# A written order for the opening of a packed-attention, MLP and MoE-attention kernel

## The chip, the cores and the metric

The kernel runs on one core of one Trainium2 chip. The metric is the device time of one execution, in microseconds. The engines are TensorE (PE, its weight loads PEld), VectorE (DVE), ScalarE (ACT), GpSimd (POOL) and SyncE (SP), which issues the DMAs in the kernel before.

## The reference, cut to what matters

```python
# packed attention: B=8, H=8 heads, S=576, D=64, 32 packed rows a head
p_packed = softmax(scale * p @ k.T) @ v            # 32 x 64 a head
x = softmax(scale * q @ p_packed.T) @ p_packed     # 576 x 64 a head, heads side by side: 576 x 512
# gated MLP, weights in float64
h = gelu_tanh(x @ w_in); u, v = h[..., :512], h[..., 512:]
v_n = (v - mean) / sqrt(var + 1e-6) * g_ln
gated = u * (w_sg @ v_n + b_sg)
x = x + gated @ w_out
# MoE of 4 attention experts, 2 of them taken by the gate of each row
w = softmax over the two largest of x @ w_gate
out = sum over e of mask * w * (causal_softmax(scale * (x wq[e]) (x wk[e]).T) @ (x wv[e]) @ wo[e])
```

## The kernel before, in words

The eight batches are run one behind the other, as a pipeline of written steps. The x of the packed attention is never formed: the second softmax (a2, 576 rows by 8 heads of 32 packed rows) is kept, and each weight that x would meet is multiplied by the packed heads instead. So `wp_mm` forms w_in times the packed heads (for v, f = 1, and for u, f = 0), `v_tiles` and `u_tile` are a2 times that, `bdw` does the same for the weights of q, k, v and the gate, and `qk` and `vlog` add a part from the gated MLP output (`qk_gated`, with w_out folded into the weights once by `fold`) and a part from a2 (`qk_packed`). Nearly all of these products are split into high and low parts (`lo_part` subtracts the high part), three passes each.

The opening (`startup`, L1129 to L1222) is batch 0 with all that is done once. w_in and w_out come as float64 words; `from_f64_top`, `from_f64_abs` and `from_f64_low` (L148 to L163) make float32 of them, five VectorE operations and one of ScalarE's for each of 12 pieces of 128 x 512. w_out is turned and folded into the q, k, v and gate weights, four pieces (`prep_w_out`, `fold`, `fold_out`); w_sg is turned and split, five pieces (`prep_w_sg`). Batch 0's k and q are turned on TensorE (`transpose_in`), those of later batches by DMA transposes of 16-bit halves, one head at a time (`turn`), stored (`keep`), read back as planes (`planes`) and joined by GpSimd (`join`). The list `TURN` holds these steps, and `tick` issues the next of them. `keep_w_all` (L217) copies the unfolded weights within DRAM in 20 DMAs, so that `load_w` can bring them back in each batch for `bdw`.

What sets the order: in `startup` only TensorE runs in the order written (`manual_schedule`, L1225); the other engines and SP's DMAs are ordered by a planner from its own costs. From L1227 on TensorE and SP follow the written order, and VectorE, ScalarE and GpSimd are the planner's. `front` (L1039) holds the v and u products, `back` (L1051) everything else of a batch, mixed with the steps of the previous batch's expert attention: S0 to S9 are scores (two heads of experts each), T0 to T9 the transposes of their softmax, y0 to y4 the products with v, o0 to o4 those with wo. Steps of the next batch's packed attention stand between them: K and Q joins, s and r the first and second packed scores, a the transposes, p and P the packed heads. All PSUM tiles come from four slots of two banks (`pd`).

Of the kernel before, what the change touches and what calls it, by code (L numbers as in the profile page):

```python
# [7 lines left out]
F32 = mybir.dt.float32  # L8
# [18 lines left out]
def packed_attention_mlp_moe_kernel(  # L27
# [35 lines left out]
    NB = {"A": 4, "B": 10, "C": 4, "D": 12, "a": 3, "p": 1, "T": 4, "nat": 2, "x": 2, "t": 4, "v2": 1, "y": 1, "W": 2}  # L63
# [44 lines left out]
    nc.sync.dma_start(g_bc, dap(moe_g_ln, 0, [[0, P], [1, DM]]))  # L108
# [39 lines left out]
    def from_f64_top(raw, dst):  # L148
        hw, top = words(raw)[:, :, 1], dst.bitcast(I32)
        nc.vector.tensor_scalar(top, hw, 3, 0x3FFFFFF8, op0=OP.logical_shift_left, op1=OP.bitwise_and)  # L150
        nc.vector.scalar_tensor_tensor(top, hw, -0x40000000, top, op0=OP.bitwise_and, op1=OP.bitwise_or)

    def from_f64_abs(raw):
        hw = words(raw)[:, :, 1].bitcast(F32)
        nc.scalar.activation(hw, hw, AF.Abs)

    def from_f64_low(raw, dst, pw):
        lw, hw, top = words(raw)[:, :, 0], words(raw)[:, :, 1], dst.bitcast(I32)
        f = pw.bitcast(F32)
        nc.vector.tensor_scalar(pw, top, -0x800000, None, op0=OP.bitwise_and)  # L160
        nc.vector.scalar_tensor_tensor(f, lw.bitcast(U32), 2.0 ** -52, f, op0=OP.mult, op1=OP.mult)
        nc.vector.tensor_tensor(f, f, dst, op=OP.add)
        nc.vector.scalar_tensor_tensor(dst, hw.bitcast(F32), LEAST_F64, f, op0=OP.is_ge, op1=OP.mult)  # L163
# [3 lines left out]
    def load_w_sg(c):  # L167
        if c < 4:
            if c % 2 == 0:
                wst["t"] = slot("A", name="wst")  # L170
            wst[c] = wst["t"][:, (c % 2) * S:(c % 2) * S + S]
        else:
            wst[c] = slot("p", name="wst")
        nc.sync.dma_start(wst[c][:TOK[c]], moe_w_sg[c * P:c * P + TOK[c], :])
# [54 lines left out]
    def prep_w_sg(c):  # L229
        n = TOK[c]  # L230
        st = wst[c]
        pw = pd("wsgT")
        pt, pl = pw[:, 0, :], pw[:, 1, :]
        for a in range(4):
            nc.tensor.transpose(pt[:, a * P:a * P + n], st[:n, a * P:(a + 1) * P], ident[:n, :n])
        nc.tensor.transpose(pl[:64, 0:n], st[:n, 512:576], ident[:n, :n])
        cols = slice(c * P, c * P + n)
        src = pt.rearrange("p (a t) -> p a t", a=4)[:, :, :n]
        act_copy(w_sg[0][:, 0:4, cols], src)
        lo_part(nc.vector, w_sg[1][:, 0:4, cols], src, w_sg[0][:, 0:4, cols])  # L240
        act_copy(w_sg[0][:64, 4, cols], pl[:64, :n])
        act_copy(w_sg[0][64:P, 4, cols], pl[:64, :n])
        lo_part(nc.vector, w_sg[1][:64, 4, cols], pl[:64, :n], w_sg[0][:64, 4, cols])
# [18 lines left out]
    woT = {}  # L262

    wos = {}

    def wo_top(c):
        wos[c] = slot("B", w=512, name="wo")
        from_f64_top(raw_out[c], wos[c])
        from_f64_abs(raw_out[c])

    def wo_low(c):
        from_f64_low(raw_out[c], wos[c], slot("t", I32, 512, name="pw"))

    def prep_w_out(c):

        wo = wos.pop(c)
        pt = pd("woT")[:, 0, :]
        for j in range(4):
# [985 lines left out]
```

## Time and profile before

| | us |
|---|---|
| median of 3 runs (lowest, highest) | 879.61 (877.87, 881.14) |
| the profiled execution | 878.9 |
| its span, first to last instruction | 877.0 |
| TensorE busy | 825.4 |
| VectorE busy | 583.3 |
| ScalarE busy | 424.7 |
| GpSimd busy | 188.4 |

The 40 slices of the page are 21.9 us each; a digit is the busy share in tenths. A busy TensorE is the modelled span of its matmuls, so it says that the stream did not stop, not that it ran at its peak. The clock row is the granted share of TensorE's full clock, in tenths.

### The profile page before, as it was taken

Reading aid. Unit: us, or ns where it says so; the run is one execution under the profiler, and the core shown is the slowest. Engines: PE = TensorE matmul, PEld = TensorE weight load, DVE = VectorE, ACT = ScalarE, POOL = GpSimd, SP = SyncE. Lnnn points to the kernel's source line nnn. Section 1 sums busy time; section 2 is a strip of 40 time slices with the busy share of each in tenths; the row PEclk is TensorE's granted clock in tenths of the full one; section 3 lists DMA queues with packets and bytes.
Section 4 is the critical chain, followed back from the end, with each engine's and each line's share of the span. In section 5 each row is a group of like instructions: output and inputs, shape, how many; then the busy total and the mean of one; then the engine's idle time right before and its main releaser. Section 6 shows DMA issues by size and latency. Waiting matters only on the chain.

```text
span 877.0 us, 19165 instructions
## 1 busy us (share of the span) xinstructions
PE 825.4 (94%) x7517; PEld 697.9 (80%) x7517; DVE 583.3 (67%) x1387; ACT 424.7 (48%) x973; POOL 188.4 (21%) x272
## 2 busy tenths in 40 slices
PE   4687988999999999999999999999999999999987
PEld 2356877788888888888789888888789888888965
DVE  6766644876577674877477665867488566866265
ACT  2356332565436542655346552655346543745245
POOL 0002051312332151303322141404222141300000
PEclk9798889999999999999999999999999999999989
DMA  9886673537445563548245563549263660100001
GB/s 307 229 208 176 143 234 86 146 88 224 114 99 143 140 188 86 154 109 231 76 130 116 148 188 83 154 111 237 69 153 89 171 178 7 74 13 26 19 1 55
DMA packets 178725, 114.08 MB, mean 130 GB/s; under 512 B 118282, under 2 KB 166666, under 8 KB 175820
## 3 DMA queue, kind: packets, MB, share of 16 engines
q1 hardware_dynamic: 178636, 112.87, 48.0%
q8 instruction: 59, 0.97, 0.5%
q14 instruction: 30, 0.25, 0.1%
HBM read 68.26 MB, written 29.63 MB: 112 GB/s over the span
## 4 chain that ended last, share of the span: by engine, by line
PE 75%; DVE 5%; ACT 2%; issue 1%; POOL 0%; ACTq 0%; DVEq 0%; POOLq 0%
PE vs L744 10%; PE qk L789 10%; PE y L968 6%; PE vlog L832 6%; PE qk L801 5%; PE v L676 5%; PE o L999 5%; PE sc L885 4%; PE u L726 4%; PE aTp L939 4%; PE vlog L836 3%; PE sc L915 2%; PE wp L625 1%; PE aTp L953 1%; PE s L448 1%
## 5 line engine op out<-in xcount | busy, mean ns | idle before, releaser
L744 PE MATMUL vs<-w_sg,vnh 128*128 128x288 f32 x512 | 92.8, 304 | 0.7 <-DVE w_sg L85 0.7
L789 PE MATMUL qk<-gh,w_qk 128*128 128x288 f32 x512 | 92.7, 304 | 0.0
L789 PEld LDWEIGHTS qk<-gh,w_qk 128*128 128x128 f32 x512 | 76.2, 193 | 10.6 <-issue 7.1
L82 ACT ACTIVATE aT<-aTp 128x512 f32<-128x512 f32 (+4 forms) x160 | 60.9, 434 | 44.1 <-PE aTp L939 36.2
L744 PEld LDWEIGHTS vs<-w_sg,vnh 128*128 128x128 f32 x512 | 75.7, 191 | 5.3 <-issue 3.0
L416 POOL COPY kT<-kp 128x576 uint16<-128x576 uint16 x56 | 48.0, 921 | 147.4 <-DMA kp<-turned_k 98.1
L898 ACT ACTIVATE at<-sc,nm 128x256 f32<-128x256 f32 (+3 forms) x128 | 66.3, 524 | 26.7 <-DVE nm L889 21.1
L691 POOL TENSOR_TENSOR rstd<-rstd,mhalf 128x1 f32<-128x1 f32 x40 | 36.4, 917 | 152.8 <-DVE rstd L690 152.8
L968 PE MATMUL y<-aT,v 128*64 128x128 f32 (+2 forms) x960 | 61.6, 267 | 0.2 <-ACT aT L82 0.2
L902 DVE TENSOR_SCALAR at<-at,sm,gw 128x256 f32<-128x256 f32 (+3 forms) x128 | 60.1, 511 | 2.3
L832 PE MATMUL vlog<-w_vg,gh 128*128 128x260 f32 (+1 forms) x320 | 60.8, 287 | 0.0
L968 PEld LDWEIGHTS y<-aT,v 128*64 128x64 f32 (+1 forms) x960 | 48.4, 140 | 14.1 <-issue 7.6
L819 POOL CAST last_q<-qk 64x64 fp32r<-64x64 f32 x64 | 14.9, 233 | 196.6 <-ACT qk L809 103.1
L789 PE MATMUL qk<-gl,w_qk 128*128 128x288 f32 x256 | 55.6, 299 | 0.0
L744 PE MATMUL vs<-w_sg,vnl 128*128 128x288 f32 x256 | 55.3, 298 | 0.0
L889 DVE TENSOR_REDUCE nm<-sc 128x2 f32<-128x256 f32 (+3 forms) x64 | 52.6, 822 | 1.7
L999 PE MATMUL o<-w_o,y 128*128 128x512 f32 x192 | 52.5, 408 | 0.5 <-ACT y L978 0.5
L832 PEld LDWEIGHTS vlog<-w_vg,gh 128*128 128x128 f32 (+1 forms) x320 | 47.4, 178 | 3.5 <-issue 2.8
L885 PE MATMUL sc<-qk 64*128 64x256 f32 (+3 forms) x384 | 47.4, 352 | 0.0
L416 POOL COPY qT<-qp 128x576 uint16<-128x576 uint16 x56 | 44.6, 870 | 11.0 <-DMA qp<-turned_q 11.0
L939 PE MATMUL aTp<-ident,at 128*128 128x128 f32 x320 | 46.6, 277 | 0.0
L899 DVE TENSOR_SCALAR sm<-sm 128x2 f32<-128x2 f32 x64 | 16.4, 256 | 44.9 <-ACT at L898 44.5
(208 smaller groups left out, 1927.9 us busy)
## 6 DMA issues: line engine op xcount, KB each, us to landing
w_in<-kept_in SPq DMA_DIRECT2D x14, 1024.0 KB
w_qk<-kept_qk SPq DMA_DIRECT2D x8, 1024.0 KB
out_dram<-ot SPq DMA_DIRECT2D x32, 256.0 KB
turned_k<-kx SPq DMA_DIRECT2D x56, 144.0 KB
turned_q<-qx SPq DMA_DIRECT2D x56, 144.0 KB
kp<-turned_k SPq DMA_DIRECT2D x56, 144.0 KB
qp<-turned_q SPq DMA_DIRECT2D x56, 144.0 KB
v<-in_v_dram SPq DMA_DIRECT2D x56, 128.0 KB
```

The costliest lines, as they stand in the source:

```text
L82: nc.scalar.activation(o, i, AF.Copy, scale=scale)
L416: nc.gpsimd.tensor_copy(w[:, i], t[:, i].rearrange("p h n -> p (h n)"))
L744: nc.tensor.matmul(pt[:, h, :HALF], s["vn", c][x][:, cols], w_sg[y][:, c, hs(h)], start=(c, x, y) == (0, 0, 0), stop=False)
L789: nc.tensor.matmul(o[:, h, :], W["w_qk"][y][:, m, cols], s["g", m][x][:, hs(h)], start=first and (m, x, y) == (0, 0, 0), stop=not first an ...
L832: nc.tensor.matmul(pt[:n, ci, :260], s["g", m][x][:, c * P:c * P + n], W["w_vg"][y][:, m, :], start=(m, x, y) == (0, 0, 0), stop=False)
L885: nc.tensor.matmul(pt[:, e, :L], qs[x][r, j * P:L], ks[y][r, :L], start=i == 0, stop=i == 2)
L889: nc.vector.tensor_reduce(nm, pt[:, :, :L], axis=AX.X, op=OP.max, negate=True)
L898: nc.scalar.activation(ats[e][:, :L], pt[:, e, :L], AF.Exp, bias=nm[:, e:e + 1], accum_out=sm[:, e:e + 1])
L902: nc.vector.tensor_scalar(ats[e][:, :L], ats[e][:, :L], sm[:, e:e + 1], s["w"][:, j, 2 * pr + e:2 * pr + e + 1], op0=OP.mult, op1=OP.mult)
L939: nc.tensor.transpose(pt[:, e, c * P:c * P + P], ats[e][:, c * P:c * P + P], ident)
L968: nc.tensor.matmul(pt[64 * e:64 * e + 64, pr * w:pr * w + w], s["v2"][:m, c, col:col + D], s["aT", pr, e, j][c][:m, :], start=c == 0, stop ...
L999: nc.tensor.matmul(pt, ys[:, pr, x, :], W["w_o"][y][:, pr, :], start=i == 0, stop=i == 5)
```

## The change

The opening becomes one list, `ORDER`, of some 300 steps, and TensorE, VectorE, ScalarE, GpSimd and SP all issue their instructions in its order. For that the functions are cut into steps of one engine each. Step names: `D...` are loads (wo and in pieces of w_out and w_in, f and piece), `...t p l g a` the parts of a conversion (upper, lower, join, guard, absolute), K, Kc, s, sm, se, n, aT, aTc, pp, ppc, ppT, ppTc, S, St, Sx, Ss, Se, Su, Sn, Sb, ah, al the packed attention of batch 0, wT, wTc, fa, fb, fh, fl the turn, fold and split of w_out, w, wh, wv, wl, wH, wL those of w_sg, wp, wph, wpl w_in times the packed heads, v, g, b, pw, c, vh, vl the v tiles, vs the products with w_sg, u, ug, go, gh, gl the gated part, `A` the first step for batch 1, `t` one tick, kw the copies within DRAM, ki the stores of converted w_in, `F` the planes of batch 1's k, `W` the reload of the q, k, v weights. Where a name ends in a small letter of the pair l/L, s/S the work is GpSimd's.

With that, GpSimd takes the join of each conversion, the subtraction of the maximum in batch 0's second softmax, and the low parts of a2, of w_sg and of the normed v in batch 0; for the last two ScalarE first writes a copy from PSUM or a scaled v to SBUF. The 20 copies within DRAM are issued on ScalarE's queue. Heads are turned in pairs, so 8 turns and 8 stores a batch for 16. Behind batch 0 `first_back`, and for later batches `later_back`, take the place of the first part of `back`: scores come in pairs (S1 S3, S5 S4, S6 S7, S8 S9, S0 S2), T1 stands behind two vs products, the second packed scores and `wp_mm` for the next v stand ahead of the last v-logit products.

```diff
-    def from_f64_low(raw, dst, pw):
...
+        def lower():
+            nc.vector.tensor_scalar(pw, top, -0x800000, None, op0=OP.bitwise_and)
+            nc.vector.scalar_tensor_tensor(f, lw.bitcast(U32), 2.0 ** -52, f, op0=OP.mult, op1=OP.mult)
+        def join(eng):
+            eng.tensor_tensor(f, f, dst, op=OP.add)
+        def guard():
+            nc.vector.scalar_tensor_tensor(dst, hw.bitcast(F32), LEAST_F64, f, op0=OP.is_ge, op1=OP.mult)
...
+        def high():
+            pt = hold["t"]
+            act_copy(copied(), pt[:, 0, :].rearrange("p (a t) -> p a t", a=4)[:, :, :n])
+            act_copy(hi[:, 0:4, cols], copied())
+            high_rest(pt)
+        def low():
+            lo_part(nc.gpsimd, lo[:, 0:4, cols], copied(), hi[:, 0:4, cols])
...
-        def turn(name, src, h):
-            x = sb.tile([P, S], U16, tag="x", name=name + "x", bufs=NB["x"])
-            nc.sync.dma_start_transpose(x, src[b, h].bitcast(U16))
...
+        def turn(name, src, j):
+            x = sb.tile([P, 2, S], U16, tag="p", name=name + "x", bufs=NB["p"])
+            rows = src[b, 2 * j:2 * j + 2].rearrange("h s d -> (h s) d").bitcast(U16)
+            nc.sync.dma_start_transpose(x.rearrange("p h s -> p (h s)"), rows)
+        def keep(name, j):
+            s[name + "x", j] = dram.tile([P, 2, S], U16, name=f"turned_{name}{b}{j}")
+            nc.sync.dma_start(s[name + "x", j], s.pop(("x", name, j)))
...
+    def v_high_0(b, c):
+        nc.scalar.activation(vg, vg, AF.Copy, scale=s.pop(("rstd", c)))
+        act_copy(hi, vg)
+    def v_low_0(b, c):
+            lo_part(nc.gpsimd, lo, vg, hi)
...
         for cs in VT:
             v_tiles(b, cs)
-            tick(2)
+            tick()
         u_tile(b, 0)
         go("T0")
-        tick()
...
+    def first_back(b, do_all):
+        tick(len(TURN))
+        do_all("K0")
+        qk_gated(b, 0, True)
+        do_all("s0 K1")
+        qk_gated(b, 2, True)
+        do_all("s1")
+        bdw(b)
+        weights(b + 1, ("in1", "in0"))
+        do_all("a0")
+        qk_packed(b, 0, False)
+        qk_out(b, 0)
+        do_all("a1 p0 Q0")
+        qk_packed(b, 2, False)
+        qk_out(b, 2)
+        keep_last_q(b, 0)
+        do_all("P0")
+        vlog(b, VT[2])
+        do_all("p1 r0 Q1 P1")
+        vlog(b, VT[1])
+        do_all("r1")
+        wp_mm(b + 1, 1)
+        ahead(b + 2)
+    def later_back(b, go, do_all):
+        go("S1 S3")
+        vs_tile(b, 0)
+        vs_tile(b, 1)
+        go("T1 T2 y0 S5 S4")
+        vs_tile(b, 2)
+        go("T3 o0 y1 T5 T4 S6 S7")
+        vs_tile(b, 3)
+        tick(len(TURN))
+        if b + 1 < B:
+            STEP.pop((b + 1, "f"))()
+        go("o1 y2")
+        bdw(b)
+        weights(b + 1, ("in1", "in0"))
+        qk(b, 0)
+        do_all("T6 o2 T7 K0 S8 S9 K1")
+        keep_last_q(b, 0)
+        qk(b, 2)
+        do_all("y3 s0 s1 T8 T9 o3 a0 a1 y4 p0 Q0 Q1 o4 P0")
+        vlog(b, VT[1])
+        do_all("p1 r0 P1")
+        vlog(b, VT[2])
+        do_all("r1")
+        if b + 1 < B:
+            wp_mm(b + 1, 1)
+        if b + 2 < B:
+            ahead(b + 2)
...
         vlog(b, VT[0])
         tick()
         gates(b)
...
-        nxt("S0" if b + 1 < B else "S8")
+        qk_packed(b, 3, True)
         tick()
-        qk_packed(b, 3, True)
-        nxt("S2" if b + 1 < B else "S6")
-        tick()
-        if b + 1 < B:
-            wp_mm(b + 1, 1)
+        nxt("S0 S2" if b + 1 < B else "S8 S6")
         qk_gated(b, 3, False)
...
+        for i, (o, x) in enumerate(keep_w_steps()):
+            Z[f"kw{i}"] = lambda o=o, x=x: nc.scalar.dma_start(o, x)
...
+    ORDER = """
+        Dwo1 Dk0 Dwo0 K0 Dp Kc0 wo1t Din11 pT wo1p wo0t wo0p pTc s0 in11t wo1a Dk1 sm0 K1 Din13 wo1l Dq0 wo0a in11p
+        se0 in13t Kc1 aT0 aTc0 Din10 s1 in13p in11l n0 sm1 Qn0 in13a se1 Qc0 in10t aT1 in13l in11a ar0 Dv0 wo0l wo1g
+        Dq1 pp0 Qn1 Dv1 n1 aTc1 Dbias wo0g ppc0 ppT0 ar1 in13g in10p in11g ppTc0 pp1 Qc1 ppc1 Din12 S0 ppT1 wT1 St0
+        in12t ppTc1 Sx0 wT0 in12p S1 Dfqk Dwo2 wTc0 in10l in12a Ss0 bi St1 fa0 wo2t Dwsg Sx1 Ss1 wTc1 Se0 w1 wo2a
+        in12l Su0 wo2p wo2l in10a Se1 w4 bj in12g wh1 wv1 wh4 w0 Dfvg fb0 wo2g wh0 w2 Sn0 wv4 fa1 Su1 Dwo3 Din03
+        Dgbc wl1 Din00 Din02 in10g Din01 Sb0 Sn1 wh2 wv0 wp1 ah0 fh0 wv2 Sb1 A wo3t w3 ah1 al0 t fb1 kw0 wph1 al1
+        fl0 kw1 wT2 wh3 wl2 wpl1 t wTc2 in01t kw2 wo3p wo3a wl0 v0 in01p g0 v1 t kw3 wv3 wo3l g1 in01l fh1 v2 g2 b0
+        b1 wl3 in01a v3 kw4 t pw0 c0 v4 pw1 fl1 kw5 wl4 vh0 fa2 wo3g vl0 kw6 t vs3_0 c1 vh1 kw7 vl1 g3 b2 in02t g4
+        wT3 t c2 b3 pw2 in02a kw8 in00t c3 vs3_1 kw9 t b4 fb2 vh2 c4 pw3 vl2 pw4 vh3 vs1_0 vs3_2 kw10 in00p vl3 t
+        in01g vs1_1 vs1_2 kw11 in00l vs1_3 wTc3 vh4 in02p vs0_0 in00a kw12 in03t vl4 t in00g vs3_3 in02l kw13 in03p
+        ki1 in03l in03a vs3_4 vs1_4 vs0_1 vk3 vs2_0 in02g kw14 in03g vk1 vs0_2 vs0_3 wp0 fh2 ki0 kw15 vs2_1 fl2 wph0
+        vs2_2 kw16 vs2_3 vs2_4 vk2 vs0_4 wpl0 F u3 kw17 ug3 u0 kw18 u2 go3 kw19 ug2 go2 ug0 u1 ug1 gh2 vk0 go1 go0
+        gh1 gh0 fa3 gl1 fb3 gh3 gl3 gl0 W fh3 gl2 fl3
+    """
     def startup():
+        steps = first()
+        for n in ORDER.split():
+            steps[n]()
...
-    with tc.manual_schedule(engines={ET.PE}):
+    with tc.manual_schedule(engines={ET.PE, ET.DVE, ET.Activation, ET.Pool, ET.SP}):
         startup()
```

## Rows read from the trace of the kernel before

**Rows 1.** The page's busy line and its slices of TensorE and its clock.
```profile
PE 825.4 (94%) x7517; PEld 697.9 (80%) x7517; DVE 583.3 (67%) x1387; ACT 424.7 (48%) x973; POOL 188.4 (21%) x272
...
PE   4687988999999999999999999999999999999987
...
PEclk9798889999999999999999999999999999999989
```

**Rows 2.** Table of stages: busy time of each engine, clock, DMA share, GB/s.
```profile
0.00:69.37 69.37, 44.60 (x336) 27.93 (x337) 45.45 (x112) 24.87 (x56) 1.66 (x12) 0.93 0.87 241
69.37:112.96 43.59, 36.39 (x234) 32.96 (x233) 32.53 (x68) 22.85 (x43) 4.60 (x5) 0.88 0.65 173
112.96:165.84 52.88, 45.78 (x483) 38.00 (x482) 28.44 (x73) 17.28 (x37) 19.58 (x30) 0.94 0.50 144
165.84:750.32 584.48, 579.94 (x5516) 497.27 (x5509) 403.80 (x955) 296.68 (x680) 156.09 (x212) 1.00 0.52 135
750.32:877.00 126.68, 118.69 (x968) 101.76 (x960) 73.05 (x182) 63.03 (x157) 6.46 (x13) 0.97 0.07 24
```

**Rows 3.** Timeline of TensorE, opening: start, length, operation, count, idle before and releaser.
```profile
12.91 1.13 PE L279 MATMUL woT<-ident,wo 128*128 128x128 f32 x4 [6.96 <-DVE wo L163]
...
36.77 5.77 PE L300 MATMUL fold<-fqk,woT 128*128 128x512 f32 x8 [7.16 <-ACT woT L82]
...
54.49 3.70 PE L300 MATMUL fold<-fqk,woT 128*128 128x512 f32 x8
...
60.56 0.70 PE L279 MATMUL woT<-ident,wo 128*128 128x128 f32 x4
...
83.60 0.66 PE L235 MATMUL wsgT<-ident,wst 64*128 64x64 f32 x4 [3.41 <-issue]
...
122.03 0.68 PE L448 MATMUL s<-kT,pT 64*32 64x288 f32 x4 [2.34 <-POOL kT L416]
...
126.24 1.16 PE L789 MATMUL qk<-gh,w_qk 128*128 128x288 f32 x4
```

**Rows 4.** Table of stages of the first 45 us, columns as in rows 2.
```profile
0.00:5.00 5.00, 0.00 (x0) 0.00 (x0) 0.72 (x19) 1.28 (x1) 1.66 (x12) 1.00 0.47 138
5.00:25.00 20.00, 12.06 (x43) 7.39 (x44) 16.75 (x31) 5.75 (x10) 0.00 (x0) 1.00 1.04 344
25.00:45.00 20.00, 11.40 (x69) 6.46 (x68) 13.24 (x31) 6.65 (x18) 0.00 (x0) 0.74 0.85 215
```

**Rows 5.** Groups by shape: count, busy us, mean ns, idle before.
```profile
L162 DVE TENSOR_TENSOR pw<-pw,w_in 128x512 f32<-128x512 f32 x8 | 5.2, 682 | 0.0
...
L85 POOL TENSOR_TENSOR a2l<-a2f,a2h 128x576 fp32r<-128x576 f32 x14 | 20.0, 1427 | 0.2
```

**Rows 6.** Timeline of SP's queue: start and length of DMA issues.
```profile
36.65 0.65 SPq L223 DMA_DIRECT2D kept_qk<-in_moe_wq_dram  x1
...
59.57 2.53 SPq L397 DMA_TRANSPOSE kx<-in_k_dram  x2
...
102.93 0.80 SPq L403 DMA_DIRECT2D turned_q<-qx  x2
```

**Rows 7.** Timeline of TensorE behind a score, in the back of batch 2.
```profile
353.17 0.79 PE L801 MATMUL qk<-a2h,bdq 128*128 128x288 f32 x4
...
354.06 0.69 PE L801 MATMUL qk<-a2h,bdq 128*128 128x288 f32 x4
```

**Rows 8.** Timelines of TensorE, VectorE and GpSimd, second softmax of batch 3.
```profile
337.42 0.72 PE L448 MATMUL s<-qT,ppT 64*32 64x288 f32 x16
...
345.12 0.81 DVE L520 STREAM_TRANSPOSE bt<-s 128x288 f32<-128x288 f32 x2
...
357.02 2.00 POOL L85 TENSOR_TENSOR a2l<-a2f,a2h 128x64 fp32r<-128x64 f32 x3
...
357.08 1.74 DVE L902 TENSOR_SCALAR at<-at,sm,gw 128x128 f32<-128x128 f32 x2
...
359.27 0.73 DVE L902 TENSOR_SCALAR at<-at,sm,gw 128x256 f32<-128x256 f32 x2
```

More of the change, by code (lines that the diff above doesn't have):

```diff
@@ L260, in prep_bias @@
         nc.vector.scalar_tensor_tensor(w_sg[1][64:66, 4, :], bb[64:66, :], sel[64:66, 0:1], sc, op0=OP.mult, op1=OP.add)
[L262 to L278, printed above, removed]
-            nc.tensor.transpose(pt[:, j * P:(j + 1) * P], wo.rearrange("p (a r) -> p r a", r=4)[:, j, :], ident)
-        t = slot("B", w=512, name="woT")
-        act_copy(t, pt)
-        woT[c] = t
@@ L303, in fold_out, with w_out_tile, fold_steps, turn @@
-    def fold_out(c):
-        pt = fpt.pop(c)
-        for i, name in enumerate(("qk", "vg")):
-            n = COLS[name]
-            hi, lo = (x[:, c, :] for x in W["w_" + name])
-            act_copy(hi, pt[:, i, :n])
-            lo_part(nc.vector, lo, pt[:, i, :n], hi)
+    def w_out_tile(c):
+        return slot("B" if c < 2 else "T", w=512, name="wo")
+    def fold_steps(c):
+        x = {}
+        def turn():
+            pt = x["t"] = pd("woT")[:, 0, :]
+            wo = w_out[c].rearrange("p (a r) -> p r a", r=4)
+            for j in range(4):
+                nc.tensor.transpose(pt[:, j * P:(j + 1) * P], wo[:, j, :], ident)
+        def turned():
+            x["w"] = w_out_tile(c)
+            act_copy(x["w"], x.pop("t"))
+        def mm(k):
+            if k == 0:
+                x["f"] = pd("fold")
+            pt = x["f"]
+            o = (pt[:, 0, :], pt[:, 1, :256], pt[:, 1, 256:260])[k]
+            o = o if k == 2 else o.rearrange("p (e d) -> p e d", d=D)
+            for j in range(4):
+                nc.tensor.matmul(o, x["w"][:, j * P:(j + 1) * P], folded[j, k], start=j == 0, stop=j == 3,
+                                 skip_group_check=True)
+        def parts():
+            if not W:
+                weight_tiles("w_qk")
+                weight_tiles("w_vg")
+            for i, name in enumerate(("qk", "vg")):
+                yield x["f"][:, i, :COLS[name]], W["w_" + name][0][:, c, :], W["w_" + name][1][:, c, :]
+        def high():
+            for p_, hi, _ in parts():
+                act_copy(hi, p_)
+        def low():
+            for p_, hi, lo in parts():
+                lo_part(nc.vector, lo, p_, hi)
+        return turn, turned, lambda: mm(0), lambda: (mm(1), mm(2)), high, low
@@ L325, in load_nat @@
     def load_nat(name, src, b, j):
[L326 to L336 removed]
+        t = nat_slot(F32, name).rearrange("p (h n) -> p h n", h=2)
@@ L667, in wp_part, with v_mm, v_gelu, v_stats @@
         return ST[b]["wp", f][x][:, Q * 512:(Q + 1) * 512]
+    def v_mm(b, pt, c):
+        s = ST[b]
+        n = 0
+        for x, y in PASSES:
+            for Q in range(2):
+                nc.tensor.matmul(pt, s["a2", Q][x][:, c * P:(c + 1) * P], wp_part(b, 1, y, Q), start=n == 0, stop=n == 5)
+                n += 1
+    def v_gelu(b, pt, c):
+        vg = ST[b]["vg", c] = slot("t", w=512, name="vg")
+        nc.scalar.activation(vg, pt, AF.Gelu_apprx_tanh)
+    def v_stats(b, c):
+        s = ST[b]
+        st = small.tile([P, 6], F32, name="bnst")
+        nc.vector.bn_stats(st, s["vg", c])
+        mv = s["mv", c] = small.tile([P, 2], F32, name="mv")
+        nc.vector.bn_aggr(mv, st)
+        rstd = s["rstd", c] = small.tile([P, 1], F32, name="rstd")
+        nc.vector.tensor_scalar(rstd, mv[:, 1:2], LN_EPS, None, op0=OP.add)
```

804 lines of the change are left out of this document (415 added, 389 removed).

## The prediction

> **What bounds the kernel now.** I read the page first: TensorE is busy for 94% of the span, and the 40 slices show where it is not: in the first seven and the last two [rows 1]. Then the table of stages: I cut it where the v products of batches 0, 1 and 7 begin (69.37, 165.84 and 750.32) and where batch 0's packed weights begin (112.96). TensorE idles 24.8 us before 69.37, 7.2 and 7.1 in the next two stages, 4.5 in the six batches that follow and 8.0 in the last stretch [rows 2]. So from 165.84 on the kernel is bound by the order of TensorE's own work, (750.32 - 165.84) / 6 = 97.41 us a batch, and 0.76 of that is idle. The opening is another regime: there TensorE waits. The timeline names for what: 6.96 us for a w_out tile that VectorE converts, 7.16 for a copy of it, 3.41 ahead of the last w_sg tile, 2.34 for k tiles that GpSimd joins [rows 3]. And it runs slowly there: eight fold products took 5.77 us from 36.77 and 3.70 us from 54.49; the granted clock's slices are lower around the first (0.74 in the mean from 25 to 45, so part of it at the lower level, 1.2 GHz) than at the second, which runs at 2.4 GHz [rows 1, 3, 4]. The DMA engines are full from 5 to 25 us [rows 4].
>
> **The change, part by part.** The sum stands against the profiled execution: 878.9 us, of which the span is 877.0. The median of the runs shown is 879.61, 0.7 more. The opening is taken in three parts.
>
> *A. Up to v of batch 0 (69.37 now).* The written list puts k, q, v and the w_in half for v ahead of the w_out and fold weights. By its tile sizes 7.8 MB stand on SP's queue up to the fold weights for q and k, 9.7 MB up to w_sg, 10.2 up to those for v. Before, 0.7 MB moved by 5 us and 6.9 MB more by 25 us, at 344 GB/s, then 215 [rows 4]. At the lower rate w_sg is there at 25 + 2.1 / 0.215 = 35 us, at the higher one at 31. Behind it TensorE has in the list four w_sg tiles (about 0.7 each by the row of the last), one and a half folds, wp and a turn of w_out, about 12 us at full clock (a fold is 60.56 - 54.49 = 6.07) [rows 3], so 47 to 49. Where the clock is low as from 36.77, a fold's q and k part costs 2.1 more, so up to 53. VectorE has about 33 us of work before the low half of wp: its 45.45 us up to 69.37 [rows 2], less 7 joins (0.68 each [rows 5]), two subtractions, the low parts of a2, two of three fold remainders and part of one conversion, plus small parts of w_sg. Some 10 us of that stand behind the first w_sg part in the list, which TensorE turns at 35 or 36 and ScalarE splits by 38: 48 again, or more where GpSimd holds it up. I take **52** for v; 47 if neither clock nor GpSimd costs, 60 if w_sg lands late and both do.
>
> *B. From v to the packed weights (43.59 now).* TensorE's 36.39 busy us [rows 2] lose the w_sg turns (some 3) and gain two folds and their turns (2 x 6.07 + 2 x 0.7): 46.9, of which about 3 are half-clock time that a denser stream would not pay: 44. Gaps were 7.2 and I take 4: **48**, from 44 (none) to 56. What covers the edits: ScalarE gets 20 DMA issues, which took SP about 0.6 us each from 36.65 on [rows 6], 12 us in all, two passes where one was for five vn tiles (3 us), two folds (2 x 1.0) and two turns (1.2), and loses the w_sg copies (5): 22.85 + 12 + 3 + 2 + 1.2 - 5 = 36 us in 48. It is in order, so each issue that stands ahead of a gelu or a split delays it by about 0.6; if this cover fails, the 12 us lie on the path. SP loses those issues. The copies' bytes stay. GpSimd's five powers (rstd) now queue behind joins and low parts of 1.4 us, and each vn tile waits for its power; the fold and vs products between are to hide that, which I count in the 4 us of gaps.
>
> The Trainium skill, page "DMA: Bandwidth & Descriptors", section "Issuing engines are not separate DMA queues", says that transfers started by different engines share the same 16 DMA engines and that only issue time is saved; by it the new queue gains no bandwidth, which is what I count, and no run so far shows a second queue here.
>
> *C. Batch 0's back (52.88 now).* Its 45.78 busy us hold 24 qk products of which most run at the half clock (1.16 for four against 0.69 [rows 3, 7], 2.4 us in all). The new order puts half a qk ahead of the first scores, so the 2.34 us of waiting for joined k go [rows 3], if the turned heads are there: eight turns of a pair at twice the 2.7 us a head of before ((102.9 - 59.6) / 16 from SP's first transpose to its last keep, [rows 6]) are 43 us from about 46, thus 90, and the k planes land at about 97, ahead of scores at about 103. On SP the planes stand behind the eight turns and behind the store of the second w_in half, which waits for VectorE's last conversion, so they can't be earlier than that. What is late next is the reload of the q and k weights, behind the last copies: about 106 against 108. **45**; 42 at best, 53 if either is late.
>
> So v of batch 1 starts at 52 + 48 + 45 = 145 in place of 165.84: 21 less.
>
> *D. The six batches after that.* Scores in pairs and the moved steps leave, by count of the written order, 47 runs of like products a batch for 57. A change of kind costs 0.1 (four products take 0.79 just behind a score and 0.69 further on [rows 7]), so 1.0 a batch, and the idle 0.76 may go [rows 2]. Against it: the second packed score now ends 17.4 us ahead of v (wp 1.0, a v-logit pair 4.3, qk 4.9, half a qk 1.8, scores 1.1, the rest of qk 3.3, wp 1.0, each as long as in this trace); its remainder a2l ended 20.9 after the first score ended (337.42 + 0.72 to 357.02 + 2.00 [rows 8]). But VectorE began the second tile only at 345.12, when the first was done, so the chain counts from the first, which is 20.5 ahead of v, and a2l is needed 1.0 later, behind four products: no stall, and none to spare. The pairs also put two softmaxes behind each other on VectorE; the two vs products (7.5) ahead of T1 and seven us ahead of T5 cover that. I take 0.7 a batch, **4** in all; ends: 10 gained, and with a stall of 2.5 a boundary 15 lost.
>
> *E. The last stretch.* Its closing order is the same and its 8 idle us stay: 0, between 2 gained and 2 lost.
>
> Sum: 878.9 - 21 - 4 = **854 us**.
>
> **Rivals.** *1, packed fully*: A 47, B 44, C 43, D 8 gained: 878.9 - 32 - 8 = 839. For it: all idle and slow stretches of the opening follow waits that an order can remove. Against: loads and conversions must come first in any order, and the first 25 us already run at full DMA share [rows 4].
>
> *2, GpSimd gives VectorE's time back.* Some 26 full-width operations move from VectorE (0.68) to GpSimd, where an a2l part takes 1.43 [rows 5]. And the trace shows them stopping VectorE: while GpSimd ran three a2l parts from 357.02, two 128 x 128 scalings took 1.74 us, and two of twice the width took 0.73 just behind [rows 8]. If each moved operation costs VectorE its whole length, its opening work goes from 45.45 + 32.53 = 78 to 78 - 18 + 26 x 1.4 = 96, from 6.7 to 103 without one other wait; with the 8 us that it waits anyway A and B end at 111, and the sum is 878.9 - 2 - 8 - 4 = 865. Against it: in-order neighbours meet for a part of the time only, and PSUM-fed steps may not be touched.
>
> The Trainium skill's page "SBUF — State Buffer", section "Who interferes with whom", makes it a rule: a VectorE operation with two SBUF inputs, or in a two-port mode, and a GpSimd one that reads SBUF exclude each other for the whole instruction. The 1.74 us agrees; in A it would cost some 5 us by that rule if half of them met.
>
> *3, ScalarE or the turned heads are late*: 12 us of issues come on the path in B, or C waits 8 for keys or weights; with one of the two 878.9 - 13 - 0 = 866. For it: turns begin later than the list's other work and SP waits at each. Against: 36 us of ScalarE in 48.
>
> *4, slower*: the a2 chain counts from the second score after all. Then v of each of seven batches waits 20.9 - 18.4 = 2.5 us, and if the clock falls behind such waits, as it shows behind the 2.34 us wait of batch 0 [rows 3], 2.4 more: 7 x 4.9 = 34 and none of D's gain: 878.9 - 21 + 34 = 892. It decides from 21 / 7 = 3 us a boundary. Against it: 345.12, above.
>
> *5, nothing of it*: the loads set the opening whatever the order, 879. Against: the share falls to 0.85 from 25 us on, and 3.41 us of idle stand at 83.60, behind all of them [rows 3, 4].
>
> **How the numbers follow.** Forecast 0.47 (its own range 846 to 862), rival 1 0.17, 2 0.15, 3 0.10, 4 0.07, 5 0.04. A range of 838 to 870 takes in 1, 2 and 3 but for their outer parts, and A's, B's and C's ends where they don't all fall together. About 0.5% (4.4 us) is what a measurement can tell from no change; faster by more than that are the forecast and rivals 1 to 3, 0.89; within it rival 5, 0.04; slower rival 4, 0.07.
>
> **What would show it.** A: v of batch 0 begins at 52, with folds 2 and 3 behind it, and GpSimd is busy from 8 us on. B: no gap above 2 us in TensorE from there to 100; ScalarE's 20 issues at 0.6 each. C: no wait for joined k. D: 96.7 from v to v. Wrong: VectorE's conversions stretched beside GpSimd (rival 2), a gap of TensorE whose releaser is ScalarE behind an issue (3), a wait for a2l at v in each batch with the clock at the half behind it (4).

## The result, and the profile after

The changed kernel took 850.94 us in the median of 4 runs (849.16 to 853.86), the kernel before 880.38 beside it; the ratio is 0.967, interval 0.963 to 0.971. Measured once more with the experiments it took 854.64 (6 runs, 850.58 to 859.33), ratio 0.973, interval 0.969 to 0.976. The forecast of 854 us lies between the two. The sum was right, but its terms were not: the opening gave 10 us in place of the 21 forecast, and the later batches and the last stretch gave 17 in place of 4. The profiled execution took 852.21 us, with a span of 850.4.

The page of the changed kernel: busy line, slices of TensorE and of its granted clock; compare [rows 1].
```profile
PE 809.0 (95%) x7517; PEld 693.3 (82%) x7517; DVE 583.6 (69%) x1358; ACT 432.8 (51%) x983; POOL 227.0 (27%) x301
...
PE   5788989899999999999999999999999999999987
...
PEclk9999999999999999999999999999999999999999
```
TensorE runs as many products (7517) in 16.4 us less busy time. Before, the clock was visibly low in the opening; here no slice falls below nine tenths. That is this execution's: a second profile of the changed kernel (experiment 9) is busy for 813.7 us, with one slice at seven tenths.

The table of stages of the changed kernel, cut like [rows 2]: v of batch 0 starts at 54.27, the transposes ahead of batch 0's packed products at 105.79, v of batch 1 at 155.99, v of batch 7 at 727.92. (Before, the second cut stood at the packed weights, which no longer come first in that stage.)
```profile
0.00:54.27 54.27, 38.99 (x309) 24.41 (x310) 42.34 (x96) 29.80 (x69) 19.81 (x27) 0.97 0.91 256
54.27:105.79 51.52, 44.02 (x262) 35.44 (x260) 39.86 (x56) 25.36 (x41) 31.31 (x27) 1.00 0.75 186
105.79:155.99 50.20, 43.69 (x484) 37.01 (x484) 28.99 (x72) 15.62 (x36) 15.47 (x24) 0.97 0.67 179
155.99:727.92 571.93, 568.48 (x5516) 497.25 (x5509) 399.16 (x952) 298.21 (x680) 153.97 (x212) 1.00 0.54 139
727.92:850.40 122.48, 113.77 (x968) 99.22 (x960) 73.29 (x186) 63.85 (x158) 6.46 (x13) 1.00 0.07 25
```
Against [rows 2] the stages gain 15.1, lose 7.9, and gain 2.7, 12.6 and 4.2: together the 26.6 us between the spans. (The second profile, cut at the same places, gains 15.1, loses 8.0, and gains 2.4, 11.9 and 1.4: 22.8.) From v to v a batch takes 571.93 / 6 = 95.32 us (97.41 before), and only 0.18 of the 2.09 saved was idle time.

TensorE's timeline in the opening and in batch 0's back, the lines with a wait (start, length, operation, idle before and releaser); they answer to [rows 3].
```profile
33.64 5.30 PE L323 MATMUL fold<-fqk,wo 128*128 128x512 f32 x8 [2.21 <-DMA fqk<-in_moe_wk_dram]
...
57.86 0.73 PE L658 MATMUL v<-wph,a2h 128*128 128x512 f32 x2 [1.95 <-ACT vg L663]
61.62 0.73 PE L658 MATMUL v<-wph,a2h 128*128 128x512 f32 x2 [0.75 <-ACT vg L663]
77.43 0.53 PE L769 MATMUL vs<-w_sg,vnl 128*128 128x288 f32 x2 [0.96 <-POOL vnl L85]
80.54 0.53 PE L773 MATMUL vs<-w_sg,vnh 128*128 128x288 f32 x2 [0.98 <-POOL vnh L85]
84.39 0.79 PE L769 MATMUL vs<-w_sg,vnh 128*128 128x288 f32 x4 [1.53 <-ACT vs L82]
99.71 3.70 PE L323 MATMUL fold<-fqk,wo 128*128 128x512 f32 x8 [1.33 <-ACT u L746]
...
116.57 0.67 PE L602 MATMUL bdv<-w_vg,ppT 64*32 64x260 f32 x16 [1.15 <-DMA w_vg<-kept_vg]
119.11 1.09 PE L494 MATMUL a1T<-ident,a 128*128 128x128 f32 x4 [1.86 <-DVE bdq L85]
...
151.03 0.62 PE L921 MATMUL sc<-qk 64*128 64x256 f32 x6 [2.40 <-DVE qk L846]
```
The waits of 6.96 and 7.16 us are gone. In their place stand many waits of 0.75 to 2.4 us, for several engines: six of them (7.5 us) between v and the packed products, and 6.5 us in batch 0's back with three smaller ones that are not shown. Behind the wait that ends at 119.11 the granted clock is at the half, 0.50 up to 122 (0.97 in the mean of that stage).

### The profile page after: what moved, and what is told of

It is laid out like the page before. It is cut to its first block, busy times and chain, and to the rows that moved or that the text cites. A ratio compares the mean times of both kernels' runs of the same rounds, so it can differ in the third digit from the quotient of the medians.

```text
span 850.4 us, 19209 instructions
## 1 busy us (share of the span) xinstructions
PE 809.0 (95%) x7517; PEld 693.3 (82%) x7517; DVE 583.6 (69%) x1358; ACT 432.8 (51%) x983; POOL 227.0 (27%) x301
## 4 chain that ended last, share of the span: by engine, by line
PE 72%; DMA 11%; DVE 8%; SPq 3%; issue 2%; ACT 2%; POOL 1%; ACTq 0%; DVEq 0%; POOLq 0%
PE vs L769 12%; PE qk L825 9%; PE vlog L868 6%; PE o L1035 5%; PE u L739 5%; PE y L1004 5%; PE v L658 5%; PE qk L837 5%; DMA qp<-turned_q 4%; PE sc L921 4%; PE aTp L975 4%; PE vlog L872 3%; PE wp L602 2%; DMA w_in<-kept_in 1%; SPq L465 1%
## 5 line engine op out<-in xcount | busy, mean ns | idle before, releaser
L472 POOL COPY kT<-kp 128x576 uint16<-128x576 uint16 x56 | 51.1, 987 | 156.0 <-DMA kp<-turned_k 156.0
L825 PE MATMUL qk<-gh,w_qk 128*128 128x288 f32 x512 | 90.6, 299 | 0.0
L1004 PE MATMUL y<-aT,v 128*64 128x128 f32 (+2 forms) x960 | 57.2, 262 | 0.8 <-ACT aT L82 0.8
L1004 PEld LDWEIGHTS y<-aT,v 128*64 128x64 f32 (+1 forms) x960 | 46.3, 136 | 13.3 <-issue 8.1
L938 DVE TENSOR_SCALAR at<-at,sm,gw 128x256 f32<-128x256 f32 (+3 forms) x128 | 55.3, 474 | 2.0
L472 POOL COPY qT<-qp 128x576 uint16<-128x576 uint16 x56 | 42.6, 833 | 47.2 <-DMA qp<-turned_q 47.1
L874 ACT ACTIVATE v<-vlog 128x512 f32<-128x512 f32 (+1 forms) x24 | 12.6, 523 | 74.9 <-PE vlog L872 74.9
L837 PE MATMUL qk<-a2h,bdq 128*128 128x288 f32 x256 | 45.6, 301 | 0.0
L868 PE MATMUL vlog<-w_vg,gl 128*128 128x260 f32 (+1 forms) x160 | 45.1, 282 | 0.0
```

Of the source, the lines that this page charges most:

```text
L472: nc.gpsimd.tensor_copy(w[:, i], t[:, i].rearrange("p h n -> p (h n)"))
L825: nc.tensor.matmul(o[:, h, :], W["w_qk"][y][:, m, cols], s["g", m][x][:, hs(h)], start=first and (m, x, y) == (0, 0, 0), stop=not first an ...
L837: nc.tensor.matmul(o[:, h, :], s["bd", Q][y][:, cols], s["a2", Q][x][:, hs(h)], start=first and (Q, x, y) == (0, 0, 0), stop=not first and ...
L868: nc.tensor.matmul(pt[:n, ci, :260], s["g", m][x][:, c * P:c * P + n], W["w_vg"][y][:, m, :], start=(m, x, y) == (0, 0, 0), stop=False)
L938: nc.vector.tensor_scalar(ats[e][:, :L], ats[e][:, :L], sm[:, e:e + 1], s["w"][:, j, 2 * pr + e:2 * pr + e + 1], op0=OP.mult, op1=OP.mult)
L1004: nc.tensor.matmul(pt[64 * e:64 * e + 64, pr * w:pr * w + w], s["v2"][:m, c, col:col + D], s["aT", pr, e, j][c][:m, :], start=c == 0, stop ...
```

## The experiments

Times are medians, and ratios are to the kernel before on the same chip.

**1. The old order of the later batches, with the new opening.**
```
-        go("S1 S3"); vs_tile(b, 0); vs_tile(b, 1); go("T1 T2 y0 S5 S4"); ...
+        go("S1"); vs_tile(b, 0); go("S3"); vs_tile(b, 1); go("T1 y0 T2 S5"); ...   # as before, to the batch's end
```


> The new opening and batch 0's back stay; batches 1 to 7 run in the order of before. Theory (the new order of the later batches is worth what the trace shows, 2.09 a batch in six batches and 4.2 in the last stretch): 850.9 + 16.7 = 867.6, between 865 and 870, with 97.4 from v to v and 79 runs of like products a batch in place of 68. Rival (the order is worth the 4 of the forecast, and the batches are shorter for another part, such as turning in pairs): 853 to 857, and v to v below 96.

866.21 us, ratio 0.987 (0.984 to 0.991). Its last two stages:
```profile
153.95:738.64 584.69, 580.30 (x5517) 497.39 (x5509) 404.58 (x956) 297.00 (x680) 157.06 (x212) 1.00 0.52 136
738.64:862.70 124.06, 115.87 (x968) 99.45 (x960) 73.07 (x182) 63.02 (x157) 6.48 (x13) 1.00 0.07 25
```
The old batch length is back: 584.69 for six batches against 584.48 in [rows 2]. So the order of the later batches, and no other part, gives the 12.6 us. In the last stretch the old order needs 124.06 us here and 126.68 in [rows 2]. The row of before has the lower clock (0.97), so 2.6 us of the 4.2 are a stretch at half clock, and 1.6 are the order. The second profile of the changed kernel (experiment 9) has such a stretch too and takes 125.27 there.

**2. GpSimd's work in the opening back on VectorE.**
```
-    ... wo1l ... in11l ... Ss0 ... al0 ... wh1 wv1 wl1 ... vh0 vl0 ...
+    ... wo1L ... in11L ... SS0 ... aL0 ... wH1 wL1 ... vH0 vL0 ...      # 41 steps
```


> In the opening the joins, subtractions and low parts that GpSimd does go back to VectorE, at the same places of the list (41 steps of the list change; ScalarE also loses the additional copies that fed GpSimd). Theory (GpSimd relieves VectorE): VectorE gets some 20 us more in front of the packed weights, where it is busy for 76 of 99.7 us now, so that it becomes the bound there: 856 to 863. Rival (GpSimd takes back by exclusion on the port what it relieves): VectorE's instructions get shorter without it, and the time is 846 to 852.

867.98 us, ratio 0.988 (0.986 to 0.991), above the end of 863 that the theory gave. Its stages, cut like those of the changed kernel:
```profile
0.00:68.07 68.07, 42.51 (x309) 26.38 (x309) 48.77 (x118) 27.43 (x66) 1.67 (x12) 0.90 0.84 238
68.07:119.45 51.38, 47.22 (x258) 37.88 (x259) 34.98 (x64) 22.08 (x35) 10.47 (x13) 0.90 0.61 154
```
and its waits ahead of v of batch 0:
```profile
53.29 6.73 PE L323 MATMUL fold<-fqk,wo 128*128 128x512 f32 x8 [5.63 <-DVE w_vg L85]
...
63.54 0.66 PE L246 MATMUL wsgT<-ident,wst 128*128 128x128 f32 x4 [2.50 <-DVE wpl L85]
```
v of batch 0 starts at 68.07, against 69.37 before: without GpSimd the new list gains almost nothing ahead of v, and v of batch 1 (171.58) is later than before (165.84). Some of this is the clock: the fold behind the wait of 5.63 takes 6.73 us where it takes 3.70 at 2.4 GHz. TensorE's busy time up to the packed products is 89.7 us against 83.0, so of the 13.7 us about 7 are slower products and 7 are waits. Whether the edit or the execution brought the slow clock is not shown. Against the two medians of the changed kernel this edit costs 13 to 17 us and that of experiment 1 costs 12 to 15, together about all that was gained. GpSimd's part in the old order of the opening was not run.

The mechanism of rival 2 is there all the same. Groups of VectorE, the conversions of w_in, in the changed kernel (mean ns of one is the number ahead of the last bar):
```profile
L156 DVE SCALAR_TENSOR_TENSOR w_in<-raw_in,w_in 128x512 int32<-128x512 int32 x8 | 8.4, 1054 | 0.3
L163 DVE SCALAR_TENSOR_TENSOR pw<-raw_in,pw 128x512 f32<-128x512 uint32 x8 | 8.3, 1036 | 0.3
...
L85 DVE TENSOR_TENSOR w_qk<-fold,w_qk 128x512 fp32r<-128x512 f32 x3 | 2.0, 680 | 0.0
...
L166 POOL TENSOR_TENSOR pw<-pw,w_in 128x512 f32<-128x512 f32 x8 | 11.4, 1428 | 19.3 <-DVE pw L163 14.2 <-issue 5.1
```
and with that work on VectorE:
```profile
L156 DVE SCALAR_TENSOR_TENSOR w_in<-raw_in,w_in 128x512 int32<-128x512 int32 x8 | 5.5, 693 | 0.3
L163 DVE SCALAR_TENSOR_TENSOR pw<-raw_in,pw 128x512 f32<-128x512 uint32 x8 | 5.5, 692 | 0.3
```
With GpSimd at work a conversion with two SBUF inputs takes 1.04 to 1.05 us in the mean, without it 0.69; the subtraction that reads PSUM (`fold`) takes 0.68 in both runs. Up to the packed products VectorE is busy for 42.34 + 39.86 = 82.2 us with GpSimd's help and 48.77 + 34.98 = 83.8 without, so the help gives back nearly all of VectorE's time. It can pay since 6.4 us of it go ahead of v of batch 0, where TensorE waits for VectorE without the help (5.63 and 2.50 above), and 4.9 come back behind it; this is read from the two stages and not shown by a run of its own. The Trainium skill's page "SBUF — State Buffer", section "Who interferes with whom", names this exclusion for two SBUF inputs; these rows agree, the PSUM row too. The rival's step from there to the end, that VectorE's sum sets the time, was wrong.

**3. Only the vn tiles back on VectorE.**
```
-    ... vh0 ... vl0 ... vh1 ... vl1 ...
+    ... vH0 ... vL0 ... vH1 ... vL1 ...      # five tiles
```


> In the opening only the five vn tiles are split on VectorE and in one pass of ScalarE, as in the later batches; the joins, the w_sg low parts and the second softmax stay on GpSimd. Theory (GpSimd's relief acts ahead of v of batch 0; between v and the packed weights VectorE has 40 of 51.5 us and can take 3.5 more): the waits of 0.96 and 0.98 for vnl and vnh go, others come, 849 to 853. Rival (VectorE is the bound there too): 854 to 857. By the exclusion of VectorE and GpSimd on the port: 845 to 848.

856.82 us, ratio 0.976 (0.973 to 0.978), so 2 to 6 more than the changed kernel's two medians and within the rival's 854 to 857. v of batch 1 comes at 159.17 (155.99 and 156.38 in its two profiles). Its stage from v of batch 0 to the packed products, and its largest wait there:
```profile
53.58:106.87 53.29, 47.20 (x261) 38.88 (x260) 39.83 (x63) 22.55 (x36) 23.16 (x22) 0.90 0.73 190
...
82.64 0.85 PE L773 MATMUL vs<-w_sg,vnh 128*128 128x288 f32 x2 [2.89 <-DVE vnh L697]
```
TensorE waits less there than in the changed kernel, 53.29 - 47.20 = 6.09 us for 7.50: two waits for VectorE's vn tiles, 0.49 and 2.89, stand where four of 0.96 to 1.53 stood. What is longer is its busy time, 47.20 for 44.02, at a clock of 0.90 for 1.00, and in batch 0's back 46.14 for 43.69, at 0.90 for 0.97. The clock is at the half behind the wait of 2.89 (0.50 from 84 to 88), but also ahead of it (0.52 from 60 to 62) and in the back, whose order is the same. So the waits do not show VectorE as the bound there, and the theory is not refuted by them; the longer time is slow clock, and whether the edit brings that stays open.

**4. The weight copies issued on SyncE.**
```
-            Z[f"kw{i}"] = lambda o=o, x=x: nc.scalar.dma_start(o, x)
+            Z[f"kw{i}"] = lambda o=o, x=x: nc.sync.dma_start(o, x)
```


> The 20 weight copies within DRAM are issued on SyncE in place of ScalarE, at the same places of the list. Theory (ScalarE's issues are covered, and on SyncE they stand ahead of the turned heads, 12 us in all): the last turned pair is stored some 8 to 12 us later than 87.9, first scores or weights of batch 0's back wait, 854 to 860. Rival (ScalarE's issues lie on the path, in the 1.95, 1.53 and 1.33 us in which TensorE waits for ScalarE from 57 to 101): 846 to 849.

851.43 us, ratio 0.971 (0.968 to 0.973): no difference, and both expectations missed. The issues take 0.54 to 0.69 us each on ScalarE, as forecast, but nothing waits for them there. On SyncE they fit into its waits between the turns: the last turned pair is stored at 82.41, even earlier than with the copies on ScalarE (87.89), and v of batch 1 is at 155.61. The late weights of the theory are there, a wait of 3.16 for w_vg, but it only takes the place of the two of 1.15 and 1.86. So who issues the copies is of no account here.

**5. Heads turned one by one.**
```
-            nc.sync.dma_start_transpose(x.rearrange("p h s -> p (h s)"), rows)
+            for h in range(2):
+                nc.sync.dma_start_transpose(x[:, h], src[b, 2 * j + h].bitcast(U16))
```


> Two transposing DMAs of one head each in place of one of a pair, into the same tile; all else stays. Theory (pairs save little: 2.4 us a head in place of 2.7): the last pair is stored at most 4 us later than 87.9, and 850.9 becomes 851 to 854. Rival (the pairs are what lets SyncE be in time for batch 0's back): scores of batch 1 wait for k, 856 or more.

856.86 us (854.65 to 861.0), ratio 0.975 (0.973 to 0.978). The last pair is stored at 90.95, 3.1 later, and v of batch 1 is at 158.14, some 2 later, with a new wait of 1.95 of the packed weights' product for the reloaded w_qk and none for k. Batch 0's back is 3.4 us longer, 1.7 of it waits and 1.7 products at a lower clock (0.94 for 0.97). From v to v nothing changes (95.32). Pairs are worth 2 us in this trace; the median's 2 to 6 does not tell this from the rival's bound.

**6. The scores of the later batches taken apart.**
```
-        go("T1 T2 y0 S5 S4")
+        go("T1 S5 T2 y0 S4")           # and S1|S3, S6|S7, S8|S9, s0|s1
```


> In batches 1 to 7 the scores that stand in pairs are taken apart (S1 and S3, S5 and S4, S6 and S7, S8 and S9, and the packed s0 and s1), which makes 6 more runs of like products a batch; the place of T1, of the packed r and wp steps and the first two scores of the next batch stay. Theory (each change of kind costs TensorE 0.17, from 1.9 busy us over 11 fewer runs): 42 changes, 7 us, 857 to 859, with no more idle time and the difference in sc and s groups. Rival 1 (0.1 a change, as the prediction had it): 855. Rival 2 (the pairs do not matter, the moved T1 and wp do): 850 to 852.

857.94 us, ratio 0.977 (0.975 to 0.980). The median suits the theory, but the trace does not. The six batches:
```profile
155.46:729.76 574.30, 571.91 (x5517) 496.84 (x5509) 397.34 (x952) 296.06 (x680) 153.50 (x212) 1.00 0.53 138
```
A batch takes 95.72 us, 0.40 more. By TensorE's sequence there are 55 changes from one kind of product to another a batch against 48 (the expectation counted 6 more), and 42 more in six batches cost 571.91 - 568.48 = 3.43 us of busy time, 0.08 each. Idle time falls by 1.06. So the forecast's 0.1 a change holds, 0.17 was wrong, and the pairs account for a fifth of the 2.09. The last stretch, with batch 7's scores, is 1.2 us longer (123.64), and v of batch 1 comes 0.5 earlier: 3.0 us in all between the two spans, where the medians differ by 3 to 7.

**7. The packed second scores next to each other again.**
```
-        do_all("... a0 a1 y4 p0 Q0 Q1 o4 P0"); vlog(b, VT[1]); do_all("p1 r0 P1"); vlog(b, VT[2]); do_all("r1")
+        do_all("... a0 a1 p0 Q0 Q1"); vlog(b, VT[2]); do_all("y4 p1 P0 o4 P1 r0 r1"); vlog(b, VT[1])
```


> In batches 1 to 6 the packed second scores r0 and r1 and the transposes P0 and P1 ahead of them stand next to each other again, as in the kernel before, with no v logits between; scores in pairs and T1's place stay. Theory (most of the 2.09 a batch comes from taking these dependent products apart: from one product's start to the next, s and ppT take 1.5 a batch less than before, though only 0.3 of that is shown as idle): 96.2 to 96.8 from v to v, 856 to 860. Rival (fewer changes of kind are the gain): two changes fewer, 95.1 to 95.4, 849 to 852.

873.72 us (12 runs), ratio 0.995 (0.993 to 0.998); 97.88 us from v to v. The direction is the theory's, the size (2.56 a batch more, for 0.9 to 1.5) about two to three times as large. The group of the packed p products, six batches, first in the changed kernel and then here (count | busy, mean ns | idle before and releasers):
```profile
L401 PE MATMUL pp<-v,a1t 128*32 128x64 f32 x384 | 8.6, 222 | 0.3 <-DMA v<-in_v_dram 0.2
```
```profile
L401 PE MATMUL pp<-v,a1t 128*32 128x64 f32 x384 | 11.9, 226 | 7.0 <-DMA v<-in_v_dram 5.6 <-ACT aT L82 1.2
```
The time from a product's start to the next product's start, summed by kind and divided by six, tells where it went (us a batch, worked out from the traces):
```
                before   after   scores apart (6)   packed together (7)
s and ppT         3.95    2.48         2.64               3.12
pp                1.88    2.04         1.93               3.57
y                 7.11    6.72         6.73               6.72
sc                7.08    6.28         7.31               6.28
qk               20.09   19.66        19.66              19.66
all others       57.30   58.14        57.45              58.53
sum              97.41   95.32        95.72              97.88
```
All other kinds together take 0.84 more in the changed kernel than before (o 0.37, aTp 0.36 and a1T 0.26 of it), so a part of what one kind gains stands at another. Of the 2.56 more in this run, 0.64 is s and ppT (0.21 more is a1T) and 1.53 is pp. In the changed kernel the second pp of a batch starts 6.5 us behind the first (318.38 and 324.84), here 5.0 (414.72 and 419.67), and v's second half, loaded once the first pp is done, is not there yet. The experiment moved two things at once, so it bounds the packed chain's own part at about 1.0 a batch (2.56 - 1.53).

**8. The back of batch 0.** One kernel puts only the second of batch 0's two scores behind half a qk; the other also spreads the packed weights and loads v's remainders once.
```
-        nxt("S0 S2" ...); qk_gated(b, 3, False)
+        nxt("S0" if b == 0 else ...); qk_gated(b, 3, False); nxt("S2") if b == 0      # both
-        do_all("s1"); bdw(b); do_all("a0"); qk_packed(b, 0, False); qk_out(b, 0); do_all("a1 p0 Q0")
+        do_all("s1 a0"); bdq_(b); do_all("a1"); qk_packed(b, 0, False); qk_out(b, 0); bdv_(b); do_all("p0 Q0")
```


> One pair alone is undone: of batch 1's, no, of batch 0's own first two scores, S0 and S2, the second goes behind half a qk. Theory (the pair made a wait of 2.41 for the PSUM tile that VectorE still reads behind the gates): the wait goes, one change of kind is added, 2.2 less, 848 to 849 where the changed kernel has 850 to 851. Rival (what is late moves on to v of batch 1): no difference.

851.25 us, ratio 0.971 (0.968 to 0.974).

> Batch 0's back alone: the first transposed softmax ahead of the packed q and k weights, the packed v weights behind the first packed qk, the second score of batch 1's pair behind half a qk; and v's remainders are loaded once and not twice in every batch (4 DMAs fewer on SyncE each). Theory (the waits in batch 0's back are the rest of what the forecast gave to C: 1.15 for w_vg, 1.86 for bdq, 0.8 for v, 2.41 for a PSUM tile at the second score, and 1.7 at the half clock): v of batch 1 at 149 to 151 in place of 156, 844 to 847. Rival (the waits move to the next product in line, since VectorE and SyncE are late as a whole): 849 to 852.

852.41 us, ratio 0.971 (0.969 to 0.973). The wait of 2.40 goes in both. Of it 1.08 comes back at v in the first, as its rival had it. The stage from the packed transposes to v of batch 1 shrinks from 50.20 to 48.64 and 47.91, and v of batch 1 is at 152.47 in both. But the whole does not differ from the changed kernel's two medians: 2.3 us cannot be told from executions that lie 10 apart.

**9. The v products in pairs in the opening, alone and with 8; the changed kernel beside them.**
```
-    ... v0 in01p g0 v1 ... v2 g2 b0 b1 wl3 in01a v3 ...
+    ... v0 v1 in01p g0 ... v2 v3 g2 b0 b1 wl3 in01a ...
```


> The changed kernel once more, unaltered, beside the others of this group. Both theories: 849 to 853; it gives the spread against which the small differences are read.

> In the opening's list the second v product of each pair stands right behind the first, ahead of its gelu (v0 v1 g0, v2 v3 g2). Theory (the 1.95 and 0.75 that TensorE waits at 57.9 and 61.6 are waits of the second half of a PSUM tile for the gelu of the first, behind a table load of 1.28 on ScalarE): both go, and as VectorE, GpSimd and ScalarE set the pace of the vn tiles behind them, half comes back: 1 to 2 less than the changed kernel beside it. Rival (vn's chain sets the end): no difference.

> The v pairs and the altered back of batch 0 together (v of batch 1 was at 152.5 there in place of 156.0). Theory (what is gained ahead of v of batch 1 is gained in the whole): v of batch 1 at 150 to 152, 845 to 848, where the changed kernel beside it has 849 to 853. Rival (the clock's half-speed stretches come back elsewhere, as the 6.8 us of them in the last stretch of that run): no difference beyond the spread.

854.64 (849 to 853 was expected), 854.88 (ratio 0.972, 0.969 to 0.974) and 854.67 (0.972, 0.970 to 0.975). The waits of 1.95 and 0.75 are gone, so they were waits for the gelu of the tile's first half. ScalarE's rows of the changed kernel show what it did meanwhile:
```profile
55.91 1.28 ACT L663 ACT_TABLE_LOAD   x1
57.21 0.60 ACT L663 ACTIVATE vg<-v 128x512 f32<-128x512 f32 x1
```
From v of batch 0 to the packed products 48.74 us remain of 51.52. Still no time is gained; in this execution v of batch 0 itself came at 59.38, though ahead of it the list is the same (start, length, idle before and releaser, as above):
```profile
47.19 1.11 PE L246 MATMUL wsgT<-ident,wst 128*128 128x128 f32 x4 [2.17 <-DVE w_sg L85]
...
48.59 6.24 PE L323 MATMUL fold<-fqk,wo 128*128 128x512 f32 x8
```
The second fold begins 2.6 us later than in the changed kernel (46.02), behind a wait for VectorE, and takes 2.5 more at the half clock (3.70 there). With the back of 8 as well, v of batch 0 was at 57.77 and v of batch 1 at 155.65. No version tried is faster than the changed kernel beyond the spread.

## Why the prediction was right or wrong

- **A, v of batch 0 at 52**: 54.27, with folds 2 and 3 behind it and GpSimd busy for 19.8 us ahead of it. Executions with this same list ahead of v show 53.6 to 59.4; the bounds of 47 and 60 held. VectorE's work was sized too low: I counted about 33 us ahead of the low half of wp, and it was busy for 40.8 before that began (52.76), with conversions that GpSimd draws out (experiment 2). The 12 us behind w_sg were added up short, too: their parts make 13.6. The reason was half right: the list alone gains 1.3 us (experiment 2), and GpSimd's part, with the clock that went with it, makes the rest.
- **B, 48**: 51.52. TensorE's work was sized well (44 forecast, 44.02 busy). The gaps are 7.5 where I took 4, and they are not one bad wait but six, for ScalarE and GpSimd. I counted in-order engines by their sums, 36 of 48 us for ScalarE, where a gelu behind a table load holds TensorE for 1.95.
- **C, 45**: 50.20. The work was right again (43.7 busy), and the waits for joined k went, as forecast. What I named as late next, the reloaded weights, cost 1.15; what I did not see were waits for VectorE as a PSUM tile's last reader (so by their releasers): 1.86 behind bdq and 2.40 at batch 0's second score. A pair of scores needs two tiles at once, and VectorE's gate steps stand ahead of the low half of qk, the last of them, two copies of 64 x 2, drawn out beside GpSimd (up to 1.29 us for one, 0.22 in the median of the kernel's sixteen):
```profile
148.49 1.68 POOL L85 TENSOR_TENSOR a2l<-a2f,a2h 128x576 fp32r<-128x576 f32 x2
148.62 1.57 DVE L909 COPY wl<-gw 64x2 f32<-64x2 f32 x2
150.22 0.76 DVE L846 SCALAR_TENSOR_TENSOR qk<-qk 128x576 fp32r<-128x576 f32 x1
```
- So v of batch 1 came at 156.0 in place of 145: the step that failed is the 21 us, of which 10 were there. A was 2.3 too low, B 3.5 and C 5.2; what is missing in B and C is in the main waits.
- **D, 4**: 12.6, above my end of 10. The count of changes (10 fewer) and their price (0.1; 0.08 measured) were right, and the pairs give 0.40 a batch after their own waits. The step that failed is that only the 0.76 of idle time was left to gain besides. Dependent products that stood next to each other hid their waits in what the profile calls busy: y0 right behind T1 took 0.97 us from start to start for eight products, and takes 0.59 with T2 between (two lines of before, then two of the changed kernel); s and ppT took 3.95 a batch, now 2.48.
```profile
286.42 1.04 PE L968 MATMUL y<-aT,v 128*64 128x128 f32 x8
287.39 0.66 PE L939 MATMUL aTp<-ident,at 128*128 128x128 f32 x4
...
274.29 0.66 PE L1004 MATMUL y<-aT,v 128*64 128x128 f32 x8
274.88 1.32 PE L921 MATMUL sc<-qk 64*128 64x384 f32 x12
```
  That the whole 12.6 comes from the order is shown (experiment 1); that the packed chain's spacing gives at most some 1.0 a batch of it is bounded (experiment 7); the split of the rest between y0, qk and the moved wp is read from the table alone.
- **E, 0**: 4.2. Batch 7's own back also runs in the new order, which I overlooked: 1.6. The other 2.6 is half clock that this execution did not have and others of the same kernel have.
- **Rival 1** (packed fully, 839) failed in the opening, and in D more was gained than its 8. **Rival 2** was right that GpSimd draws VectorE's instructions out, and wrong in its size (96 us of VectorE's work up to the packed products, 82.2 measured) and its end. **Rival 3**: issues on ScalarE cost nothing (experiment 4); heads stored 3.1 us later cost 1.7 of waits (experiment 5). **Rival 4**: as forecast the a2 chain counts from the first score, since VectorE begins the second tile only as the first is done. That step and the chain's last on GpSimd, batch 3:
```profile
333.14 0.81 DVE L519 STREAM_TRANSPOSE bt<-s 128x288 f32<-128x288 f32 x2
...
343.43 1.70 POOL L85 TENSOR_TENSOR a2l<-a2f,a2h 128x576 fp32r<-128x576 f32 x2
```
It ends at 345.13, ahead of v at 346.58 and 2.5 us ahead of the products that need it (347.61), where the forecast had none to spare. TensorE does not wait there.

The total was right by luck, because two mis-sized terms cancelled: 11 too much for the opening and 13 too little for what follows (12 and 9 by the second profile).

## What to carry to other kernels

Busy time in a profile can hold short stalls between dependent products, as it did here, so measure a kind of work from start to start, and compare with the same products elsewhere in the trace, before taking the idle column for all there is to gain. Moving work from a full engine to a slower one can pay with no gain in busy time, if what it shortens is ahead of the wait and what it lengthens is behind it. When large waits go from an opening, price what comes next as a number of small waits for several engines, tiles' last readers among them, and not as the largest one left.

## What the runs showed of the hardware that was not expected

- The same list ahead of v of batch 0 ended between 53.6 and 59.4 us in different executions. Stretches at the half clock fall on different products, and a second fold then takes 4.69 to 6.24 us in place of 3.70. The mean of the clock does not tell the end: at 0.87 ahead of v (experiment 4) v came at 54.33, at 1.00 (experiment 3) at 53.58, and at 0.94 (the v pairs) at 59.38, where half of the delay stands behind a wait for VectorE. The last stretch has one in some executions (125.27) and not in others (122.48). Two medians of the changed kernel lie 3.7 us apart, so differences below some 4 us are not told by medians of five here.
- A table load of 1.28 us stands ahead of the first gelu of the opening (0.60), and together they make TensorE wait 1.95 us with a tile's second half. The Trainium skill's page "ScalarE: Activation LUTs", section "What ACT_TABLE_LOAD costs", has 1283 ns for it, which agrees; it adds 1.38 us for a drain, which these rows do not show apart: the load starts at 55.91, as the instruction ahead of it (55.22, 0.68 long) ends, and the gelu follows at 57.21.
